# Decode attention on one core: value matmuls with the probabilities as stationary operand, and the maximum of a head taken ahead of the exponentials

## The chip, the cores and the metric

The kernel runs on one core of a Trainium2 chip. The metric is the device time of one execution in microseconds (us). The time of a kernel is the median of several runs; profiles come from one execution of their own. Engines are named as in the profile: PE (TensorE; PEld is its weight load), DVE (VectorE), ACT (ScalarE), POOL (GpSimd) and SP (SyncE, which here issues transfers). SBUF is the working memory, PSUM the memory that matmuls write.

## The reference, cut to what matters

A batch of 8 single tokens attends to a window of 2048 cached positions, with 32 query heads that share 8 K and V heads, and a small gated block scales the result:

```python
xn = _layernorm(x)                                   # x: 8 x 1 x 512
q = (xn @ wq).reshape(8, 1, 32, 128)
k = repeat(k_cache[:, :, -2048:, :], 4)              # cache: 8 x 8 x 8192 x 128, bf16
v = repeat(v_cache[:, :, -2048:, :], 4)
p = softmax(einsum("bhqd,bhkd->bhqk", q, k) * 128 ** -0.5)
s = einsum("bhqk,bhkd->bhqd", p, v).reshape(8, 1, 4096) @ wo
h = sigmoid(xn @ w_gate) * (xn @ w_up)               # 512 to 1792
return x + s * silu(h @ w_down)
```

All inputs are bf16. The windows of K and V are 67.1 MB of the 81.0 MB that are read, each element once.

## The kernel before, in words

**Tiles and transfers.** The K and the V window of one batch are each two tiles of four heads (2.1 MB a tile): 128 partitions hold 4 heads times 32 stretches of positions, and a partition holds 64 consecutive positions of 128 numbers. There are five K buffers and four V buffers. All loads go through SP's queue in one fixed order (`want_rows`, `want_cache`, lines 134 to 148): the block's weights and wq first, then K and V tiles in turn with V three tiles behind K, and wo in four pieces at the end, in K buffers. `pump` issues the head of that list as soon as its pool has room; a head without room holds up all that follow. `free` is called where the last instruction that reads a tile is emitted: for K after the last transpose of the tile, for V after the last value matmul on it.

**A batch** is handled in 16 steps of the loop at line 535; a unit `u` is two steps, four units make one K tile. In each step PE transposes eight 128x128 blocks of K (`k_transposes`, L343) and DVE copies them from PSUM (L348). `scores` (L362) multiplies them by the queries, in four column groups of the array, one for each K head: a query operand of 32 columns per head, 512 positions per matmul. A row of the score tile (128 x 512) is thus one head and one of four parts of its positions (index `j`), so a head is spread over four rows.

**Softmax before.** `row_max` (L376, L378) takes the maximum of each row, and ACT forms the exponentials of each row against this own maximum (L385), with the row's sum. `p_transposes` (L399, L404) turns the probabilities so that positions lie on the partitions. The four rows of a head have different maxima: `stat_rows`, `stat_weights`, `stat_sums` and `stat_factors` bring maxima and sums onto one partition, compute a factor for each row (L409 to L455), and `spread_factors` (L465, L473) copies the factors to all partitions by an fp32 matmul.

**Values before.** `values` (L485) handles one unit: 16 matmuls, each with a 128x128 block of V as the stationary operand and 16 columns of probabilities as the moving one, summed in PSUM. Each row has a result of its own; `normalise` (L499 to L516) multiplies by the factors, adds the four rows of a head and spreads the result, and `turn` (L526, L533) brings it into the layout of the output projection `fin` (L577). That projection runs once, after all batches: 128 matmuls in four column groups, then two DVE operations (L589, L591) and the store.

**Order of the work.** It is written out by hand (`manual_schedule`): the dictionary `tasks` says which functions are emitted in which step, after that step's K transposes, and each engine runs its instructions in that order. While batch b is loaded and scored, the row maxima of batch b-1 stand at step 2, its probabilities are turned at steps 8 and 9, its first V tile is used at steps 12 to 15, and the second V tile of batch b-2 at steps 5 to 8. So the first V tile of a batch comes free at step 15 of the next batch and the second at step 8 of the one after. After the last batch the loop makes one more round without K.

Of the kernel before, what the change touches and what calls it, by code (L numbers as in the profile page):

```python
# [10 lines left out]
def kernel(  # L11
# [13 lines left out]
    nc = tc.nc  # L25
# [90 lines left out]
    def free(tag):  # L116
        room[tag] += 1
        pump()
# [36 lines left out]
    make_identity(nc, ident[:])  # L155
    ident_f = consts.tile([P, P], f32, name="ident_f")
    make_identity(nc, ident_f[:])
    ones_row = consts.tile([1, P], f32, name="ones_row")
    nc.gpsimd.memset(ones_row[:], 1.0)

    perm = consts.tile([P, P], bf16, name="perm")
    nc.vector.tensor_copy(
# [157 lines left out]
            ),  # L320
        )


    free("k")
    free("k")

    oT_ps = ps_o.tile([P, 2, P], f32, name="oT_ps")

    kT = {}
    s_ps = {}  # L330
    pT = {}
    st = {}
    row = {}
    fac = {}

    def k_transposes(b, u, h):
        i, j = u // NJ, u % NJ
# [32 lines left out]
            )  # L370

    def row_max(b):
        st[b] = small.tile([P, 2], f32, name="st")
        nc.vector.reduce_max(out=st[b][:, 0:1], in_=s_ps[b][:], axis=AX.X)  # L376
        nb = small.tile([P, 1], f32, name="nb")
        nc.vector.tensor_scalar(  # L378
            out=nb[:], in0=st[b][:, 0:1], scalar1=-scale, scalar2=None, op0=ALU.mult
        )  # L380

        s = s_ps.pop(b)
        for l in range(G):
            rows = slice(NR * l, NR * (l + 1))
            nc.scalar.activation(  # L385
                out=p_buf[b % 2][rows, :, l, :],
                in_=s[rows, :].rearrange("k (c p) -> k p c", p=PG),
                func=AF.Exp,
                bias=nb[rows, :],
                scale=scale,  # L390
                accum_out=st[b][rows, 1:2],
            )

    def p_transposes(b, h):
        if h == 0:
            pT[b] = ppool.tile([P, CU, P], bf16, name="pT_sb")
        pT_ps = ps_t.tile([P, CH, P], bf16, name="pT_ps", tag="t")
        for c in range(CH):
            nc.tensor.transpose(  # L399
                out=pT_ps[:, c, :],  # L400
                in_=p_buf[b % 2][:, :, :, h * CH + c].rearrange("k p l -> k (p l)"),
                identity=ident[:],
            )
        nc.vector.tensor_copy(out=pT[b][:, h * CH : (h + 1) * CH, :], in_=pT_ps[:])  # L404

    def stat_rows(b):
        r = ps_m.tile([1, 2, P], f32, name="r_ps", tag="m")
        for k in range(2):
            nc.tensor.transpose(  # L409
                out=r[:, k, :], in_=st[b][:, k : k + 1], identity=ident_f[:]  # L410
            )
        row[b] = r
        del st[b]

    NH = NQ * rep

    def stat_weights(b):
        r = row[b]
        top = small.tile([1, G, NH], f32, name="top")
        nc.vector.reduce_max(  # L420
            out=top[:],
            in_=r[:, 0, :].rearrange("o (l j h) -> o l h j", l=G, j=NJ),
            axis=AX.X,
        )
        d = small.tile([1, G, NJ, NH], f32, name="d")
        nc.vector.tensor_tensor(  # L426
            out=d[:],
            in0=r[:, 0, :].rearrange("o (l j h) -> o l j h", l=G, j=NJ),
            in1=top[:].unsqueeze(2).to_broadcast([1, G, NJ, NH]),
            op=ALU.subtract,  # L430
        )
        w = small.tile([1, G, NJ, NH], f32, name="w")
        nc.scalar.activation(out=w[:], in_=d[:], func=AF.Exp, scale=scale)  # L433
        row[b] = (r, w)

    def stat_sums(b):
        r, w = row[b]
        wd = small.tile([1, G, NJ, NH], f32, name="wd")
        nc.vector.tensor_tensor(
            out=wd[:],  # L440
            in0=w[:],
            in1=r[:, 1, :].rearrange("o (l j h) -> o l j h", l=G, j=NJ),
            op=ALU.mult,
        )
        den = small.tile([1, G, NH], f32, name="den")
        nc.vector.reduce_sum(
            out=den[:], in_=wd[:].rearrange("o l j h -> o l h j"), axis=AX.X
        )
        row[b] = (w, den)

    def stat_factors(b):
        w, den = row[b]
        nc.vector.reciprocal(out=den[:], in_=den[:])
        f = small.tile([1, G, NJ, NH], f32, name="f")
        nc.vector.tensor_tensor(  # L455
            out=f[:],
            in0=w[:],
            in1=den[:].unsqueeze(2).to_broadcast([1, G, NJ, NH]),
            op=ALU.mult,
        )  # L460
        row[b] = f

    def spread_factors(b):
        f_ps = ps_m.tile([P, P], f32, name="f_ps", tag="m")
        nc.tensor.matmul(  # L465
            f_ps[:],
            lhsT=ones_row[:],
            rhs=row.pop(b)[:].rearrange("o l j h -> o (l j h)"),
            start=True,
            stop=True,  # L470
        )
        fac[b] = small.tile([P, P], f32, name="fac")
        nc.scalar.copy(out=fac[b][:], in_=f_ps[:])  # L473

    def values(b, u):
        i, j = u // NJ, u % NJ
        v_sb = v_tiles[(b, i)]

        def cols(ap):
            return ap.rearrange("p (l j i r) -> p l j i r", l=G, j=NJ, i=NQ)[  # L480
                :, :, j, i, :
            ]

        for c in range(CU):
            nc.tensor.matmul(  # L485
                cols(oT_ps[:, b % 2, :]),
                lhsT=v_sb[:, j * CU + c, :],
                rhs=cols(pT[b][:, c, :]),
                start=(c == 0),
                stop=(c == CU - 1),  # L490
            )
        if j == NJ - 1:
            del v_tiles[(b, i)]
            free("v")

    def normalise(b):
        del pT[b]
        t = small.tile([P, G, NJ, NQ, rep], f32, name="on")
        nc.vector.tensor_tensor(  # L499
            out=t[:].rearrange("p l j i r -> p (l j i r)"),  # L500
            in0=oT_ps[:, b % 2, :],
            in1=fac.pop(b)[:],
            op=ALU.mult,
        )
        oT = small.tile([P, Hq], bf16, name="oT")
        with nc.allow_low_precision(reason="operand of the next matmul"):
            for i in range(NQ):
                nc.vector.reduce_sum(  # L508
                    out=oT[:, i * G * rep : (i + 1) * G * rep].rearrange(
                        "p (l r) -> p l r", l=G  # L510
                    ),
                    in_=t[:, :, :, i, :].rearrange("p l j r -> p l r j"),
                    axis=AX.X,
                )
        oB = small.tile([P, Hq, NDQ], bf16, name="oB")
        nc.vector.tensor_tensor(  # L516
            out=oB[:],
            in0=oT[:].unsqueeze(2).to_broadcast([P, Hq, NDQ]),
            in1=band[:].unsqueeze(1).to_broadcast([P, Hq, NDQ]),
            op=ALU.mult,  # L520
        )
        row[b] = oB

    def turn(b):
        oP_ps = ps_m.tile([P, RT], f32, name="oP_ps", tag="m")
        nc.tensor.matmul(  # L526
            oP_ps[:],
            lhsT=row.pop(b)[:].rearrange("p h q -> p (h q)"),
            rhs=pick[:],
            start=True,  # L530
            stop=True,
        )
        nc.scalar.copy(out=oP_sb[:, :, b], in_=oP_ps[:])  # L533

    for b in range(B + 1):
        now = b if b < B else None
        pb = b - 1 if b >= 1 else None
        pp = b - 2 if b >= 2 else None
        tasks = {s: [] for s in range(2 * NU + 1)}
        if now is not None:  # L540
            for u in range(NU - 1):
                tasks[2 * u + 3].append(lambda u=u: scores(now, u))
        if pb is not None:
            tasks[1].append(lambda: scores(pb, NU - 1))
            tasks[2].append(lambda: row_max(pb))
            tasks[8].append(lambda: p_transposes(pb, 0))
            tasks[9].append(lambda: p_transposes(pb, 1))
            tasks[8].append(lambda: stat_rows(pb))
            tasks[9].append(lambda: stat_weights(pb))
            tasks[11].append(lambda: stat_sums(pb))  # L550
            tasks[12].append(lambda: stat_factors(pb))
            if b < B:
                tasks[15].append(lambda: spread_factors(pb))
            for u in range(NJ):
                tasks[12 + u].append(lambda u=u: values(pb, u))
        if pp is not None:
            for u in range(NJ, NU):
                tasks[5 + u - NJ].append(lambda u=u: values(pp, u))
            tasks[9].append(lambda: normalise(pp))
            tasks[13].append(lambda: turn(pp))  # L560
        for s in range(2 * NU + 1):
            if now is not None and s < 2 * NU:
                k_transposes(now, s // 2, s % 2)
            for f in tasks[s]:
                f()
    spread_factors(B - 1)
    for u in range(NJ, NU):
        values(B - 1, u)
    normalise(B - 1)
    turn(B - 1)  # L570

# [55 lines left out]
```

## Time and profile before

| what | value |
|---|---|
| median of 3 runs | 203.11 us (202.01 to 203.39) |
| the profiled execution | 202.38 us, span 200.2 us, mean granted clock 0.88 |
| PE, PEld | 155.0 us (77%), 124.0 us (62%) |
| DVE, ACT | 129.6 us (65%), 38.2 us (19%) |
| K transposes L343 / their copies L348 | 76.9 / 83.4 us |
| value matmuls L485, weight loads | 34.8 us x1024, 31.5 us |
| scores L362 | 26.2 us x256 |
| transfers | 81.41 MB, mean 407 GB/s |

The span is the profiled part of an execution; the execution's own time is 2.2 us longer. In the rows of slices each digit is the busy share of one fortieth of the span, in tenths; PEclk is the clock that PE was granted, in tenths of full speed. In the chain, a line has the start, the length and what ran, and the chain is followed back from the last instruction. The mean time of one matmul in a group is its time from start to end, while matmuls overlap: what a matmul adds in a stream is read from the chain or from the length of a group divided by its number.

### The profile page before, as it was taken

The page shows a single profiled execution, that of the slowest core. Times are in us where ns is not written, and L with a number is a line of the kernel's source. Part 1 is how long each engine was busy: PE and PEld are TensorE (multiplying, and loading weights), DVE is VectorE, ACT ScalarE, POOL GpSimd, SP SyncE. Part 2 cuts the span into 40 slices and gives each one's busy share as a digit, 9 for nine tenths or more (in the row PEclk, how much of TensorE's full clock was granted, in tenths as well). Part 3 has the DMA queues.
Part 4 walks back from the last instruction along what each step waited for, and adds up shares of the span by engine and source line. Part 5 has one row for each costly group of instructions (what it writes and reads, how often), then busy time and mean ns, then how long its engine had stood idle before and what let it go on. Part 6 is the DMA issues. An engine that isn't in the chain of part 4 may idle for free.

```text
span 200.2 us, 6209 instructions
## 1 busy us (share of the span) xinstructions
PE 155.0 (77%) x2838; PEld 124.0 (62%) x2838; DVE 129.6 (65%) x272; ACT 38.2 (19%) x97; POOL 1.3 (1%) x9
## 2 busy tenths in 40 slices
PE   0397057999699989878987998889688978885763
PEld 0144057676577877667766876767477767765662
DVE  4824005899698798838873887697549873961621
ACT  5040000004402401601060106010501060023100
POOL 2000000000000000000000000000000000000000
PEclk9999555899999999979997899999969996995558
DMA  6999999999999999999999999999999999999940
GB/s 211 438 424 438 432 425 425 439 429 424 425 429 435 422 429 425 429 435 425 432 422 429 439 422 425 425 432 429 429 425 425 432 435 422 425 425 425 419 195 7
DMA packets 6009, 81.41 MB, mean 407 GB/s; under 512 B 728, under 2 KB 736, under 8 KB 864
## 3 DMA queue, kind: packets, MB, share of 16 engines
q1 hardware_dynamic: 5936, 81.01, 95.3%
q8 instruction: 22, 0.36, 0.7%
q14 instruction: 3, 0.02, 0.0%
q10 hardware_dynamic: 48, 0.01, 0.0%
HBM read 81.01 MB, written 0.01 MB: 405 GB/s over the span
## 4 chain that ended last, share of the span: by engine, by line
DMA 70%; PE 18%; DVE 6%; ACT 2%; SPq 2%; issue 1%; ACTq 0%; DVEq 0%
DMA k_sb<-in_A_k_cache_dram 70%; PE kT_ps L343 8%; PE oT_ps L485 3%; PE pT_ps L399 2%; PE s_ps L362 2%; DVE kT_sb L348 2%; PE fin_ps L577 2%; ACT p_buf L385 2%; SPq L99 1%; DVE pT_sb L404 1%; DVE st L376 1%; PE r_ps L409 1%; PE f_ps L465 1%; DVE oT L508 0%; DVE on L499 0%
## 5 line engine op out<-in xcount | busy, mean ns | idle before, releaser
L348 DVE COPY kT_sb<-kT_ps 128x1024 bf16<-128x1024 bf16 x128 | 83.4, 683 | 27.3 <-PE kT_ps L343 26.8
L343 PE MATMUL kT_ps<-perm,k_sb 128*128 128x128 bf16 x1024 | 76.9, 227 | 9.9 <-DMA k_sb<-in_A_k_cache_dram 9.9
L343 PEld LDWEIGHTS <-k_sb 128*128 128x128 bf16 x1024 | 62.4, 102 | 17.6 <-DMA k_sb<-in_A_k_cache_dram 10.5
L485 PEld LDWEIGHTS <-v_sb 128*128 128x128 bf16 x1024 | 31.5, 98 | 9.1 <-issue 6.2
L485 PE MATMUL oT_ps<-pT_sb,v_sb 128*128 128x16 bf16 x1024 | 34.8, 171 | 2.5 <-DVE on L499 1.5
L362 PE MATMUL s_ps<-kT_sb,qm_sb 128*32 128x512 bf16 x256 | 26.2, 399 | 7.0 <-DVE kT_sb L348 6.2
L385 ACT ACTIVATE p_buf<-s_ps,nb 32x512 bf16<-32x512 f32 x32 | 21.7, 679 | 24.0 <-DVE nb L378 23.7
L404 DVE COPY pT_sb<-pT_ps 128x1024 bf16<-128x1024 bf16 x16 | 11.0, 689 | 10.6 <-PE pT_ps L399 10.6
L399 PE MATMUL pT_ps<-ident,p_buf 128*128 128x128 bf16 x128 | 13.4, 262 | 4.6 <-ACT p_buf L385 4.6
L362 PEld LDWEIGHTS <-qm_sb 128*32 128x32 bf16 x256 | 8.3, 93 | 13.5 <-issue 6.4
L399 PEld LDWEIGHTS <-p_buf 128*128 128x128 bf16 x128 | 11.0, 156 | 6.8 <-ACT p_buf L385 4.8
L433 ACT ACTIVATE w<-d 1x128 f32<-1x128 f32 x8 | 2.5, 309 | 50.2 <-DVE d L426 50.2
L308 PE MATMUL qT_ps<-xnT_sb,wq_sb 128*128 128x8 bf16 x128 | 3.7, 168 | 7.0 <-DMA wq_sb<-in_A_wq_dram 7.0
L308 PEld LDWEIGHTS <-wq_sb 128*128 128x128 bf16 x128 | 3.6, 104 | 7.3 <-DMA wq_sb<-in_A_wq_dram 7.3
L233 PE MATMUL g_ps<-wg_sb,xnT_sb 128*8 128x448 bf16 x16 | 5.3, 509 | 3.2 <-DMA wg_sb<-in_B_w_gate_dram 3.2
L316 DVE CAST qm_sb<-qT_ps 128x32 bf16<-128x32 f32 x8 | 0.9, 182 | 10.2 <-PE qT_ps L308 10.2
L385 ACT ACT_TABLE_LOAD x1 | 1.3, 1283 | 27.7 <-DVE nb L378 27.7
L533 ACT CAST oP_sb<-oP_ps 128x32 bf16<-128x32 f32 x8 | 2.4, 300 | 21.0 <-PE oP_ps L526 21.0
L385 ACT ACTIVATION_READ_ACCUMULATOR p_buf<-s_ps,nb 32x1 f32 x32 | 5.9, 184 | 0.0
L376 DVE TENSOR_REDUCE st<-s_ps 128x1 f32<-128x512 f32 x8 | 5.5, 682 | 0.5 <-PE s_ps L362 0.5
L233 PEld LDWEIGHTS <-xnT_sb 128*8 128x8 bf16 x16 | 1.8, 115 | 6.3 <-issue 5.6
L473 ACT COPY fac<-f_ps 128x128 f32<-128x128 f32 x8 | 2.1, 266 | 17.2 <-PE f_ps L465 17.2
(62 smaller groups left out, 71.9 us busy)
## 6 DMA issues: line engine op xcount, KB each, us to landing
k_sb<-in_A_k_cache_dram SPq DMA_DIRECT2D x16, 2048.0 KB, 36.5
v_sb<-in_A_v_cache_dram SPq DMA_DIRECT2D x16, 2048.0 KB, 33.2
wq_sb<-in_A_wq_dram SPq DMA_DIRECT2D x2, 2048.0 KB
wo_sb<-in_A_wo_dram SPq DMA_DIRECT2D x2, 1024.0 KB, 21.4
wg_sb<-in_B_w_gate_dram SPq DMA_DIRECT2D x1, 1792.0 KB, 7.4
wu_sb<-in_B_w_up_dram SPq DMA_DIRECT2D x1, 1792.0 KB
wd_sb<-in_B_w_down_dram SPq DMA_DIRECT2D x1, 1792.0 KB
wo_sb<-in_A_wo_dram SPq DMA_DIRECT2D x1, 1536.0 KB, 19.7
```

The costliest lines, as they stand in the source:

```text
L233: nc.tensor.matmul(g_ps[:], lhsT=xnT_sb[:, kt, :], rhs=weights[("wg_sb", kt)][:, k * FC : (k + 1) * FC], start=(kt == 0), stop=(kt == KT - 1),
L308: nc.tensor.matmul(qT_ps[:, h * B : (h + 1) * B], lhsT=weights[("wq_sb", kt)][:, h * Dh : (h + 1) * Dh], rhs=xnT_sb[:, kt, :], start=(kt = ...
L343: nc.tensor.transpose(out=kT_ps[:, c, :], in_=k_sb[:, j * CU + h * CH + c, :], identity=perm[:],)
L348: nc.vector.tensor_copy(out=kT[(b, u)][:, h * CH : (h + 1) * CH, :], in_=kT_ps[:])
L362: nc.tensor.matmul(s_ps[b][NR * l : NR * (l + 1), :], lhsT=qm_sb[:, b, i * G + l, o : o + Z], rhs=t[:, :, PG * l : PG * (l + 1)], start=(u ...
L376: nc.vector.reduce_max(out=st[b][:, 0:1], in_=s_ps[b][:], axis=AX.X)
L385: nc.scalar.activation(out=p_buf[b % 2][rows, :, l, :], in_=s[rows, :].rearrange("k (c p) -> k p c", p=PG), func=AF.Exp, bias=nb[rows, :], ...
L399: nc.tensor.transpose(out=pT_ps[:, c, :], in_=p_buf[b % 2][:, :, :, h * CH + c].rearrange("k p l -> k (p l)"), identity=ident[:],)
L404: nc.vector.tensor_copy(out=pT[b][:, h * CH : (h + 1) * CH, :], in_=pT_ps[:])
L433: nc.scalar.activation(out=w[:], in_=d[:], func=AF.Exp, scale=scale)
L485: nc.tensor.matmul(cols(oT_ps[:, b % 2, :]), lhsT=v_sb[:, j * CU + c, :], rhs=cols(pT[b][:, c, :]), start=(c == 0), stop=(c == CU - 1),)
L577: nc.tensor.matmul(fin_ps[Z * j : Z * (j + 1), :], lhsT=oP_sb[:, t, :], rhs=weights[("wo_sb", t)][:, j * P : (j + 1) * P], start=(t == 0), ...
```

## The change

It changes the softmax's statistics, the value matmuls and the order of both.

- The maximum of a head, over its four rows, is formed ahead of the exponentials: DVE takes the row maxima, PE turns them onto one partition (`stat_rows`), DVE takes the maximum of four and scales it, an fp32 matmul with one column brings it back to the rows (`spread_max`), and ACT copies it and then forms the exponentials. All rows of a head now share one scale, and the factors per row are gone.
- The sums of the rows are added and spread by an fp32 matmul against ones (`sums`), in one layout with the result.
- A value matmul has the probabilities as the stationary operand (32 columns: the rows of one tile and two of the four parts) and 256 columns of V as the moving one: two position blocks side by side, of which the rows of the fitting part are used. Four such matmuls, one in each column group of the array, cover both V tiles of a batch at one `c`; 16 values of `c` make a batch. The transposes of the probabilities take a permuted identity (`turn_rows`), which sorts the rows into those groups.
- The result lies with rows on partitions. `combine` copies it from PSUM on ACT, and `normalise` adds the four rows of a head and turns the result by two fp32 matmuls with a selection matrix (`sel_out`). Both matrices and `turn_rows` are made once, on DVE.
- In the order of the work, the statistics of batch b-1 stand at steps 2, 4 and 6 (before: 8 to 15), its turned probabilities at 11 and 12, and all values of batch b-2 at steps 6 to 13, after which both of its V tiles come free. The round after the last batch is written out; there the values of the last batch are formed one tile after the other.

```diff
+    Hh = G * rep
+    turn_rows = consts.tile([P, P], bf16, name="turn_rows")
+    sel_den = consts.tile([P, Hq], f32, name="sel_den")
+    sel_out = consts.tile([P, 2, Hq], f32, name="sel_out")
...
-    oT_ps = ps_o.tile([P, 2, P], f32, name="oT_ps")
+    o_ps = ps_o.tile([P, 2, 2 * Dh], f32, name="o_ps")
+    m_ps = ps_m.tile([P, 2, 256], f32, name="m_ps", tag="m")
...
     def row_max(b):
-        st[b] = small.tile([P, 2], f32, name="st")
-        nc.vector.reduce_max(out=st[b][:, 0:1], in_=s_ps[b][:], axis=AX.X)
+        st[b] = small.tile([P, 1], f32, name="st")
+        nc.vector.reduce_max(out=st[b][:], in_=s_ps[b][:], axis=AX.X)
+
+    def stat_rows(b):
+        nc.tensor.transpose(out=r_ps[b % 2], in_=st.pop(b)[:], identity=ident_f[:])
+        top = small.tile([1, G, NH], f32, name="top")
+        nc.vector.reduce_max(
+            out=top[:],
+            in_=r_ps[b % 2].rearrange("o (l j h) -> o l h j", l=G, j=NJ),
+            axis=AX.X,
+        )
+        row[b] = small.tile([1, G, NJ, NH], f32, name="neg")
+        nc.vector.tensor_scalar(
...
+        )
+
+    def spread_max(b):
+        nc.tensor.matmul(
+            nb_ps[b % 2],
+            lhsT=row.pop(b)[:].rearrange("o l j h -> o (l j h)"),
+            rhs=ones_sq[0:1, 0:1],
+            start=True,
+            stop=True,
+        )
         nb = small.tile([P, 1], f32, name="nb")
-        nc.vector.tensor_scalar(
-            out=nb[:], in0=st[b][:, 0:1], scalar1=-scale, scalar2=None, op0=ALU.mult
-        )
+        nc.scalar.copy(out=nb[:], in_=nb_ps[b % 2])
...
-                identity=ident[:],
+                identity=turn_rows[:],
...
-    def stat_weights(b):
...
-    def stat_sums(b):
...
-    def stat_factors(b):
...
-    def spread_factors(b):
...
-    def values(b, u):
...
+    def sums(b):
+        own = small.tile([P, Hq], f32, name="own")
+        nc.vector.tensor_scalar(
+            out=own[:],
+            in0=sel_den[:],
+            scalar1=st.pop(b)[:],
+            scalar2=None,
+            op0=ALU.mult,
+        )
+        nc.tensor.matmul(
+            den_ps[b % 2], lhsT=ones_sq[:], rhs=own[:], start=True, stop=True
+        )
+        den = small.tile([P, Hq], f32, name="den")
+        nc.vector.reciprocal(out=den[:], in_=den_ps[b % 2])
+        inv[b] = small.tile([P, Hq, NDQ], f32, name="inv")
...
+    def values(b, c, tiles=range(NQ)):
+        for i in tiles:
+            v = v_tiles[(b, i)][:].rearrange("p (m e c) d -> p m c e d", e=2, c=CU)
+            for m in range(NJ // 2):
+                k = i * (NJ // 2) + m
+                rows = slice(32 * k, 32 * (k + 1))
+                nc.tensor.matmul(
+                    o_ps[rows, b % 2, :].rearrange("k (e d) -> k e d", e=2),
+                    lhsT=pT[b][:, c, rows],
+                    rhs=v[:, m, c],
+                    start=(c == 0),
+                    stop=(c == CU - 1),
+                    tile_position=(0, 32 * k),
+                    skip_group_check=True,
+                )
+            if c == CU - 1:
+                del v_tiles[(b, i)]
+                free("v")
+
+    def combine(b):
...
+        nc.scalar.copy(
+            out=o[:], in_=o_ps[:, b % 2, :].rearrange("k (e d) -> k e d", e=2)
+        )
...
     def normalise(b):
...
+        for e in range(2):
             nc.tensor.matmul(
...
+                oT_ps[b % 2],
+                lhsT=o[:, e, :],
+                rhs=sel_out[:, e, :],
+                start=(e == 0),
+                stop=(e == 1),
+            )
...
+            tasks[2].append(lambda: row_max(pb))
+            tasks[4].append(lambda: stat_rows(pb))
+            tasks[6].append(lambda: spread_max(pb))
+            tasks[11].append(lambda: p_transposes(pb, 0))
+            tasks[12].append(lambda: p_transposes(pb, 1))
+            tasks[13].append(lambda: sums(pb))
         if pp is not None:
+            for c in range(CU):
+                tasks[6 + c // 2].append(lambda c=c: values(pp, c))
+            tasks[14].append(lambda: combine(pp))
+            tasks[15].append(lambda: normalise(pp))
+        if b >= 3:
+            tasks[1].append(lambda: turn(b - 3))
...
+    scores(B - 1, NU - 1)
+    turn(B - 3)
+    row_max(B - 1)
+    for c in range(CU):
+        if c == CU // 4:
+            stat_rows(B - 1)
+        if c == CU // 2:
+            spread_max(B - 1)
+        values(B - 2, c)
+    combine(B - 2)
+    p_transposes(B - 1, 0)
+    p_transposes(B - 1, 1)
+    normalise(B - 2)
+    sums(B - 1)
+    turn(B - 2)
+    for i in range(NQ):
+        for c in range(CU):
+            values(B - 1, c, (i,))
+    combine(B - 1)
     normalise(B - 1)
     turn(B - 1)
```

More of the change, by code (lines that the diff above doesn't have):

```diff
@@ L157 @@
     make_identity(nc, ident_f[:])
-    ones_row = consts.tile([1, P], f32, name="ones_row")
-    nc.gpsimd.memset(ones_row[:], 1.0)
+    ones_sq = consts.tile([P, P], f32, name="ones_sq")
+    nc.gpsimd.memset(ones_sq[:], 1.0)
     perm = consts.tile([P, P], bf16, name="perm")
@@ L325 @@
     free("k")
-    oT_ps = ps_o.tile([P, 2, P], f32, name="oT_ps")
+    Hh = G * rep
[3 more added lines that the diff above has]
+    for i in range(NQ):
+        nc.vector.tensor_copy(
+            out=turn_rows[:].rearrange("k (i j l r) -> k i j l r", i=NQ, j=NJ, l=G)[
+                :, i
+            ],
+            in_=ident[:].rearrange("k (l j i r) -> k i j l r", i=NQ, j=NJ, l=G)[:, i],
+        )
+        nc.vector.reduce_sum(
+            out=sel_den[:, i * Hh : (i + 1) * Hh].rearrange("k (l r) -> k l r", l=G),
+            in_=ident_f[:].rearrange("k (l j i r) -> k i l r j", l=G, j=NJ, i=NQ)[:, i],
+            axis=AX.X,
+        )
+    for e in range(2):
+        nc.vector.reduce_sum(
+            out=sel_out[:, e, :].rearrange("k (i h) -> k i h", i=NQ),
+            in_=ident_f[:].rearrange(
+                "k (i m e h) -> k e i h m", i=NQ, m=NJ // 2, e=2
+            )[:, e],
+            axis=AX.X,
+        )
+    o_ps = ps_o.tile([P, 2, 2 * Dh], f32, name="o_ps")
+    m_ps = ps_m.tile([P, 2, 256], f32, name="m_ps", tag="m")
+    r_ps = [m_ps[0:1, x, 0:P] for x in range(2)]
+    nb_ps = [m_ps[:, x, 128:129] for x in range(2)]
+    den_ps = [m_ps[:, x, 136 : 136 + Hq] for x in range(2)]
+    oT_ps = [m_ps[:, x, 168 : 168 + Hq] for x in range(2)]
+    oP_ps = [m_ps[:, x, 200 : 200 + RT] for x in range(2)]
     kT = {}
@@ L333 @@
     row = {}
-    fac = {}
+    inv = {}
     def k_transposes(b, u, h):
@@ L370, in scores @@
             )
+    NH = NQ * rep
     def row_max(b):
-        st[b] = small.tile([P, 2], f32, name="st")
-        nc.vector.reduce_max(out=st[b][:, 0:1], in_=s_ps[b][:], axis=AX.X)
+        st[b] = small.tile([P, 1], f32, name="st")
[6 more added lines that the diff above has]
+            in_=r_ps[b % 2].rearrange("o (l j h) -> o l h j", l=G, j=NJ),
+            axis=AX.X,
+        )
+        row[b] = small.tile([1, G, NJ, NH], f32, name="neg")
+        nc.vector.tensor_scalar(
+            out=row[b][:],
+            in0=top[:].unsqueeze(2).to_broadcast([1, G, NJ, NH]),
+            scalar1=-scale,
+            scalar2=None,
[9 more added lines that the diff above has]
+        )
         nb = small.tile([P, 1], f32, name="nb")
-        nc.vector.tensor_scalar(
-            out=nb[:], in0=st[b][:, 0:1], scalar1=-scale, scalar2=None, op0=ALU.mult
-        )
+        nc.scalar.copy(out=nb[:], in_=nb_ps[b % 2])
         s = s_ps.pop(b)
+        st[b] = small.tile([P, 1], f32, name="sums")
         for l in range(G):
@@ L390, in row_max @@
                 scale=scale,
-                accum_out=st[b][rows, 1:2],
+                accum_out=st[b][rows, :],
             )
@@ L401, in p_transposes @@
                 in_=p_buf[b % 2][:, :, :, h * CH + c].rearrange("k p l -> k (p l)"),
-                identity=ident[:],
+                identity=turn_rows[:],
             )
         nc.vector.tensor_copy(out=pT[b][:, h * CH : (h + 1) * CH, :], in_=pT_ps[:])
[L406 to L413, printed above, removed]
@@ L415 @@
-    NH = NQ * rep
-    def stat_weights(b):
[L418 to L423, printed above, removed]
-        )
-        d = small.tile([1, G, NJ, NH], f32, name="d")
-        nc.vector.tensor_tensor(
[L427 to L434, printed above, removed]
@@ L436, in stat_sums @@
-    def stat_sums(b):
[L437 to L442, printed above, removed]
+    def sums(b):
[4 more added lines that the diff above has]
+            scalar1=st.pop(b)[:],
+            scalar2=None,
+            op0=ALU.mult,
+        )
+        nc.tensor.matmul(
[4 more added lines that the diff above has]
+        inv[b] = small.tile([P, Hq, NDQ], f32, name="inv")
+        nc.vector.tensor_tensor(
+            out=inv[b][:],
+            in0=den[:].unsqueeze(2).to_broadcast([P, Hq, NDQ]),
+            in1=band[:].unsqueeze(1).to_broadcast([P, Hq, NDQ]),
@@ L443, in stat_sums @@
             op=ALU.mult,
         )
-        den = small.tile([1, G, NH], f32, name="den")
-        nc.vector.reduce_sum(
-            out=den[:], in_=wd[:].rearrange("o l j h -> o l h j"), axis=AX.X
-        )
-        row[b] = (w, den)
-    def stat_factors(b):
[L452 to L461, printed above, removed]
@@ L463, in spread_factors @@
-    def spread_factors(b):
[L464 to L473, printed above, removed]
-    def values(b, u):
[L476 to L490, printed above, removed]
-            )
-        if j == NJ - 1:
-            del v_tiles[(b, i)]
-            free("v")
@@ L496, in normalise @@
[L496 to L514, printed above, removed]
+    def values(b, c, tiles=range(NQ)):
[16 more added lines that the diff above has]
+                free("v")
@@ new lines, in combine, with normalise @@
+    def combine(b):
+        del pT[b]
+        o = small.tile([P, 2, Dh], f32, name="o_sb")
+        nc.scalar.copy(
+            out=o[:], in_=o_ps[:, b % 2, :].rearrange("k (e d) -> k e d", e=2)
+        )
+        row[b] = o
+    def normalise(b):
+        o = row.pop(b)
+        for e in range(2):
+            nc.tensor.matmul(
+                oT_ps[b % 2],
[3 more added lines that the diff above has]
+                stop=(e == 1),
+            )
@@ L517, in normalise @@
             out=oB[:],
-            in0=oT[:].unsqueeze(2).to_broadcast([P, Hq, NDQ]),
-            in1=band[:].unsqueeze(1).to_broadcast([P, Hq, NDQ]),
+            in0=oT_ps[b % 2].unsqueeze(2).to_broadcast([P, Hq, NDQ]),
+            in1=inv.pop(b)[:],
             op=ALU.mult,
@@ L524, in turn @@
     def turn(b):
-        oP_ps = ps_m.tile([P, RT], f32, name="oP_ps", tag="m")
         nc.tensor.matmul(
-            oP_ps[:],
+            oP_ps[b % 2],
             lhsT=row.pop(b)[:].rearrange("p h q -> p (h q)"),
@@ L532, in turn @@
         )
-        nc.scalar.copy(out=oP_sb[:, :, b], in_=oP_ps[:])
-    for b in range(B + 1):
-        now = b if b < B else None
+        nc.scalar.copy(out=oP_sb[:, :, b], in_=oP_ps[b % 2])
+    for b in range(B):
         pb = b - 1 if b >= 1 else None
         pp = b - 2 if b >= 2 else None
[L539 to L542, printed above, removed]
+        tasks = {s: [] for s in range(2 * NU)}
+        for u in range(NU - 1):
+            tasks[2 * u + 3].append(lambda u=u: scores(b, u))
         if pb is not None:
@@ L545 @@
             tasks[2].append(lambda: row_max(pb))
[L546 to L555, printed above, removed]
-        if pp is not None:
[L557 to L563, printed above, removed]
+            tasks[4].append(lambda: stat_rows(pb))
[3 more added lines that the diff above has]
+            tasks[13].append(lambda: sums(pb))
+        if pp is not None:
+            for c in range(CU):
[4 more added lines that the diff above has]
+            tasks[1].append(lambda: turn(b - 3))
+        for s in range(2 * NU):
+            k_transposes(b, s // 2, s % 2)
             for f in tasks[s]:
                 f()
-    spread_factors(B - 1)
-    for u in range(NJ, NU):
-        values(B - 1, u)
+    scores(B - 1, NU - 1)
[13 more added lines that the diff above has]
+    turn(B - 2)
+    for i in range(NQ):
+        for c in range(CU):
+            values(B - 1, c, (i,))
+    combine(B - 1)
     normalise(B - 1)
```

## The prediction, made before the changed kernel ran

> **What bounds the kernel now.** I read the slices of the page first, then the chain that ended last, then the last microseconds by window.
>
> ```profile
> PEclk9999555899999999979997899999969996995558
> DMA  6999999999999999999999999999999999999940
> ...
> HBM read 81.01 MB, written 0.01 MB: 405 GB/s over the span
> ```
>
> The DMA row stands at 9 from the second slice to the 38th: the 16 engines are full from about 5 to 190 us, and PE, at 77%, waits for them. Where it waits is in the chain:
>
> ```profile
> 128.06 37.99 DMA k_sb<-in_A_k_cache_dram
> ...
> 166.10 1.03 PE kT_ps L343 x8
> ...
> 179.12 0.77 ACT p_buf L385 x2
> ...
> 189.53 1.82 PE oT_ps L485 x64
> ...
> 193.19 3.63 PE fin_ps L577 x96
> ```
>
> The last K tile lands at 166.05. From there the chain is compute: transposes and scores, the last exponentials (179.12 to 182.25), value matmuls (to 191.35), the output projection (193.19 to 196.82); another 3.4 us end the span. But the transfers end at almost the same time:
>
> ```profile
> wo_sb<-in_A_wo_dram SPq DMA_DIRECT2D x1, 512.0 KB, 25.0
> ```
>
> This last piece of wo is issued at 171.0, so it lands at 196.0. The windows agree:
>
> ```profile
> 195.00:196.00 1.00, 1.00 (x48) 1.00 (x44) 0.00 (x0) 0.00 (x0) 0.00 (x0) 0.50 0.13 33
> 196.00:197.00 1.00, 0.79 (x32) 0.52 (x20) 0.16 (x1) 0.00 (x0) 0.00 (x0) 0.63 0.00 0
> ```
>
> Columns here are PE, PEld, DVE, ACT, POOL, clock, DMA share, GB/s. The projection takes 3.63/128 = 28.4 ns a matmul; its last 16, on that piece, take 0.45 us, so no order of the compute could end before 196.45. That is 0.37 us ahead of what was measured: **two ends of nearly equal length**. A change in compute can gain a few tenths and lose without limit.
>
> **The change, part by part.** First the stream of transfers. Four V buffers hold two batches. Before, they come free at step 15 of the next batch and step 8 of the one after; now both at step 13 of the one after, and SP is one queue in fixed order, so K tiles wait behind them. From K tile to K tile is 9.9 us (the K waits of the chain end at 86.2, 125.7 and 166.05, two batches or 39.7 us apart). At the step 8 whose K tile has just landed, four tiles (V, K, V, K; 19.8 us) are still issued. Before, steps 8 to 13 took 166.1 to 174.8, cold start included; so new issues come 8.8 us later, with 11 us queued. **Cost in the middle: nothing.** If a batch took over 19.8 us of compute this cover would shrink, but PE now rests 1.5 to 2 us a batch.
>
> At the end of the list only V of batch 6 follows the last K. 12.58 MB in 166.05 to 196.0 is 420 GB/s, so those two tiles land at 176.0. V of batch 7 and wo, issued from 168.86 on before, now wait for step 13 of batch 7: I get 175.0, plus 0.54 (an issue on SP), plus about 1 us to the first data (estimate: first issue at 0.74, windows near full rate from 3 us on, so 0.5 to 2). Bubble 0.5 us, bounds 0 and 2. New floor: 196.45 + 0.5 = 196.95.
>
> In the loop, PE loses 128 value matmuls a batch (28 to 31 ns each by the chain, 3.8 us) and gets 64 of 256 columns, in fours. The nearest row is L362, four 512-column matmuls in four column groups: 0.33 us by the chain. Half of that bounds a four of 256 columns at 0.17 us, the projection's rate (4 x 28.4 ns for 128 columns at clock 0.50) gives 0.11 at full clock: 16 fours are 1.8 to 2.7 us. Four fp32 matmuls and one transpose (nearest row f_ps, 0.41 us a pair of passes) replace one and two; DVE drops seven operations of 0.26 to 0.37 (d, wd, den's sum, f, on, two oT) and gets own and inv at about 0.28. So a batch gains about 1 us, and nothing comes of it: the next K tile is not there earlier. The exponentials start at step 6 instead of 2, 3.1 us, done ahead of the transposes now at 11. The first exponentials now wait for DVE, PE, DVE, PE, ACT; behind spread_max on PE stand step 7's transposes, with K's wait as cover. Behind the wait of the sums matmul for own (DVE, after a 0.68 us copy) stand the last values of step 13, hence V's release: 0.7 us, in my 175.0. Six small DVE operations at the start (about 1.4 us) fit between 31.57, the end of the casts, and the first copy at 33.05. Nothing.
>
> Whether switching between tiled and untiled matmuls costs anything: 0.33 us for a four against 4 x 28.4 x 4 / 2 = 0.23 leaves at most 0.10 us a visit; eight visits a batch are 0.8 us, inside the cover, and the tail has three more, 0.3 us, of which I take none. The Trainium skill, TensorEngine Tiling (Array Packing), Key Properties, says that changing the tiling mode drains TensorE; by that rule the sum would be up to 0.3 us higher, and the 0.10 us neither shows nor excludes it.
>
> **The end of the compute**, from 166.1. Steps 8 to 13 to 174.9: six groups of K transposes (two cold at 1.0, four at 0.5), three scores (0.33, cold 0.45), six value groups (0.23, cold 0.45), two pT groups (0.51), the 0.7 wait and the sums' 0.3, with 0.5 in waits for DVE. Steps 14 and 15, scores and normalise to 177.4: 0.7 earlier than the 178.1 before. Row maximum 0.7 (178.15). Then new: transpose and its latency 0.35, top 0.27, neg 0.28, matmul 0.3, copy 0.25: exponentials start at 179.6 and end at 182.75, **0.5 later** than before. pT 2.0 (1.07 + 0.92 by the chain, cold), normalise 0.9, oB and own 0.5, sums 0.4, turn 0.2: value matmuls of batch 7 start at 186.75. There the new form is dear: a tile at a time, so only two of four column groups work. 32 pairs of 256 columns by the projection's rate are 32 x 0.227 = 7.3 us at clock 0.50 and 3.6 at full, against 128 x 28 ns = 3.6 before, whose time did not hang on the clock. The clock rows decide:
>
> ```profile
> 32.00:33.00 1.00, 1.00 (x10) 1.00 (x11) 0.00 (x0) 0.00 (x0) 0.00 (x0) 0.50 1.07 459
> ...
> 36.00:37.00 1.00, 1.00 (x19) 0.95 (x16) 0.48 (x2) 0.00 (x0) 0.00 (x0) 0.84 0.96 410
> ...
> 190.00:191.00 1.00, 1.00 (x44) 1.00 (x41) 0.00 (x0) 0.00 (x0) 0.00 (x0) 0.50 0.81 336
> ```
>
> After a rest the clock came back 4.2 us into dense work (31.98 to 36.2) and 3.5 into the projection; the 16-column matmuls up to 191.35 did not bring it back. PE rests from 180.2 to 182.75 for the exponentials, so I start values cold, full after 4.2 us: 4.2 + (1 - 4.2/7.3) x 3.6 = 5.7 us, to 192.5. (The Trainium skill, TensorE: Matmul & The Clock Gate, Part 1, has one free-running window of about 3.4 us; by that the wait lies between 3.4 and 6.8 us and values take 5.4 to 7.1; the trace's 3.5 and 4.2 fit.) Then copy 0.45, normalise 0.8, oB 0.3, turn 0.2, cast 0.3, gaps 0.3: projection from 194.85. At 3.63 us cold or 1.8 at full clock; after 2.4 us of near rest I take 3.2. End 198.05 against 196.82: **+1.2 us**, above the floor. Span 201.4; with the 2.2 us outside the span (202.38 - 200.2) the profiled execution becomes 203.6. The median of the runs shown stands 0.7 above it, so **204.3 us**. About 1% (2 us) is what a measurement of this kernel can tell from no change.
>
> **Rivals.**
> - The tail hides. Clock back at once and kept: values 3.9, projection 1.8, end 194.7, then the last wo piece decides at 196.95: 203.1 to 203.4. For it: pT and normalise ahead of the values are nearly dense. Against: the same stretch ran at 0.50 before. 0.22.
> - Slower. The clock stays at half through values and projection: values to 194.1, projection from 196.5 to 200.1: +3.3, 206.4. It decides once PE's rest between 180 and 183 takes the clock and the work up to 190.2 is too thin to return it: slices 37 to 39 of the page are 5 5 5. 0.22.
> - Slower too: transfers starve. V released late in every batch costs the stream what is beyond the 11 us; 1 us in each of five batches is 208. Against: PE's rests. 0.07.
> - The stream itself gets quicker, or the projection ends at the floor on a stream without bubble (202.7). A time under 201.1 needs an end at 194.8, before the last weights have landed at 420 GB/s. 0.04.
> - My forecast, 203.4 to 205.5: 0.45.
>
> That the change does not do what it says I hold small: the maximum is shared ahead of the exponentials and row factors go, in any case.
>
> **Numbers.** Range 202.6 to 207.0: from the stream's floor with the spread of the runs, up past the cold rival with fp32 matmuls at the cold 0.76 of f_ps. Faster by over 1% 0.04; within, 0.58 (the hidden tail and most of the forecast); slower 0.38 (the two slow rivals, and the upper end of the forecast).
>
> **What would show it.** DMA at 9 through slice 37, and the waits for K about 39.7 us apart: the middle is free. SP issuing V of batch 7 at about 175, not 169; last exponentials ending near 182.8; the last value stage 5 to 7 us long with the clock at 0.50 in its first part; projection ending near 198. Wrong if PE waits for V inside a batch, if fp32 matmuls on the tail take over 0.8 us each, or if the last K tile lands later than 167.

## The result, and the profile after

The changed kernel takes 203.66 us (median of 16 runs, 203.37 to 206.28) against 202.71 for the kernel before (16 runs, 202.01 to 203.82): a ratio of **1.0063**, 95% interval 1.0033 to 1.0092. That is slower, and within the 1% that the prediction took as no change. The profiled execution took 203.39 us with a span of 201.2, 1.0 us more than before on both counts.

The slices of the changed kernel, in the order of the page:

```profile
PEclk9999555899999999969997999999958999996678
DMA  6999999999999999999999999999999999499980
GB/s 215 430 425 436 433 420 436 430 427 422 430 440 423 427 427 436 423 427 436 423 427 427 443 420 433 433 414 433 427 436 420 433 436 410 186 414 410 426 370 5
```

In the DMA row the 35th slice, 171 to 176 us, is a 4 (186 GB/s) where there was a 9. The 39th is an 8 where there was a 4, since the transfers end later. Up to the 34th slice the stream is as full as before, and PE waited for K about as long as before. The first line is the kernel before, the second the changed one (time in all, times, longest):

```profile
PE kT_ps L343 <- DMA k_sb<-in_A_k_cache_dram: 9.9, 7, 2.2
```

```profile
PE kT_ps L376 <- DMA k_sb<-in_A_k_cache_dram: 10.4, 6, 2.5
```

The chain that ended last, in order of time, shows what that hole does (start, length, what ran):

```profile
146.12 0.05 issue
146.16 1.03 PE kT_ps L376 x8
...
173.70 0.33 PE o_ps L495 x8
174.03 1.01 PE kT_ps L376 x16
175.05 0.20 SPq L89
...
176.99 20.30 DMA wo_sb<-in_A_wo_dram
197.29 0.04 issue
197.33 0.43 PE fin_ps L598 x16
```

Before, the chain ran through the last exponentials, the value matmuls and the projection. Now it leaves PE at 175: the last value matmuls of step 13 (L495, 173.70 to 174.03) release the V tiles, SP issues the last V tiles and wo, and the chain ends with the landing of wo at 197.29, 1.3 us later than the 196.0 of before. In both kernels 16 matmuls need that last piece. From 146.16 to 175 the chain is compute without a wait for K, so the pace of the compute from the middle of batch 6 on sets the time of the release. In the timeline of the same stretch, PE stands waiting in the middle of the projection (the bracket is idle time, and what ended it):

```profile
185.76 5.20 PE L495 MATMUL o_ps<-v_sb,pT_sb 128*32 128x256 bf16 x64
193.07 2.21 PE L598 MATMUL fin_ps<-wo_sb,oP_sb 128*32 128x128 bf16 x80 [0.39 <-ACT oP_sb L543]
196.11 0.87 PE L598 MATMUL fin_ps<-wo_sb,oP_sb 128*32 128x128 bf16 x32 [0.82 <-DMA wo_sb<-in_A_wo_dram]
197.33 0.41 PE L598 MATMUL fin_ps<-wo_sb,oP_sb 128*32 128x128 bf16 x16 [0.35 <-DMA wo_sb<-in_A_wo_dram]
```

The projection starts at 193.07, 0.12 us earlier than before (193.19). Without the two waits, the 3.63 us that the projection took before would have ended at 196.7, where the kernel before ended (196.82). The compute is not longer; the transfers end later.

The windows around the hole (the last three columns are clock, DMA share, GB/s):

```profile
171.00:172.00 1.00, 1.00 (x21) 0.72 (x20) 0.99 (x2) 0.00 (x0) 0.00 (x0) 1.00 0.65 279
172.00:173.00 1.00, 0.69 (x11) 0.29 (x8) 0.90 (x2) 0.00 (x0) 0.00 (x0) 1.00 0.55 229
173.00:174.00 1.00, 0.71 (x11) 0.46 (x12) 0.50 (x3) 0.00 (x0) 0.00 (x0) 1.00 0.31 131
174.00:175.00 1.00, 1.00 (x24) 0.90 (x20) 0.76 (x3) 0.37 (x1) 0.00 (x0) 1.00 0.08 33
175.00:176.00 1.00, 0.96 (x13) 0.71 (x12) 0.95 (x3) 0.00 (x0) 0.00 (x0) 1.00 0.88 262
```

From 171 on the DMA share falls from window to window, as it would if one DMA engine after another ran out of work; at 174 to 175 it is that of little more than one of 16. SP's first issue is at 174.06, and in windows of 0.2 us nothing moves from 174.4 to 175.4; then the stream starts again.

So there are two readings. **Theory A**: the late release of V in the last batch decides, and nothing else in the change costs time. **Theory B**, the forecast's own: the new form of the value matmuls and what follows it lengthen the compute at the end, and the landing of wo comes second. In this one profile A's end is 1.1 us later than B's (197.76 against 196.7), about as much as the whole change in time, so it needs a test.

### The profile page after: what moved, and what is told of

It reads as the page before. It is cut to its first block, busy times and chain, and to the rows that moved or that the text cites. A ratio compares the mean times of both kernels' runs of the same rounds, so it can differ in the third digit from the quotient of the medians.

```text
span 201.2 us, 5246 instructions
## 1 busy us (share of the span) xinstructions
PE 157.6 (78%) x2366; PEld 110.4 (55%) x2366; DVE 122.9 (61%) x238; ACT 37.9 (19%) x97; POOL 1.3 (1%) x9
## 4 chain that ended last, share of the span: by engine, by line
DMA 67%; PE 25%; SPq 3%; DVE 3%; issue 1%
DMA k_sb<-in_A_k_cache_dram 57%; PE kT_ps L376 14%; DMA wo_sb<-in_A_wo_dram 10%; PE o_ps L495 5%; PE s_ps L395 3%; PE pT_ps L458 2%; SPq L99 2%; DVE kT_sb L381 2%; SPq L89 1%; PE m_ps L475 1%; DVE st L410 0%; DVE own L468 0%; PE m_ps L519 0%; PE fin_ps L598 0%; PE m_ps L430 0%
## 5 line engine op out<-in xcount | busy, mean ns | idle before, releaser
L376 PE MATMUL kT_ps<-perm,k_sb 128*128 128x128 bf16 x1024 | 78.5, 228 | 10.4 <-DMA k_sb<-in_A_k_cache_dram 10.4
L495 PE MATMUL o_ps<-v_sb,pT_sb 128*32 128x256 bf16 x512 | 28.3, 304 | 0.0
L495 PEld LDWEIGHTS <-pT_sb 128*32 128x32 bf16 x512 | 12.3, 102 | 6.6 <-issue 2.3
L511 ACT COPY o_sb<-o_ps 128x256 f32<-128x256 f32 x8 | 3.0, 372 | 58.8 <-PE o_ps L495 58.8
L458 PE MATMUL pT_ps<-turn_rows,p_buf 128*128 128x128 bf16 x128 | 11.0, 230 | 3.6 <-ACT p_buf L444 3.6
L458 PEld LDWEIGHTS <-p_buf 128*128 128x128 bf16 x128 | 9.3, 150 | 5.6 <-ACT p_buf L444 4.1
L395 PEld LDWEIGHTS <-qm_sb 128*32 128x32 bf16 x256 | 6.7, 93 | 7.0 <-issue 0.8
L475 PE MATMUL m_ps<-own,ones_sq 128*128 128x32 f32 x16 | 3.5, 302 | 5.2 <-DVE own L468 5.2
L475 PEld LDWEIGHTS m_ps<-own,ones_sq 128*128 128x128 f32 x16 | 2.6, 203 | 7.4 <-DVE own L468 7.4
L527 DVE TENSOR_TENSOR oB<-m_ps,inv 128x128 bf16<-128x128 f32 x8 | 2.3, 292 | 6.6 <-PE m_ps L519 6.2
L543 ACT CAST oP_sb<-m_ps 128x32 bf16<-128x32 f32 x8 | 2.4, 301 | 21.1 <-PE m_ps L536 21.1
```

The costliest lines, as they stand in the source:

```text
L376: nc.tensor.transpose(out=kT_ps[:, c, :], in_=k_sb[:, j * CU + h * CH + c, :], identity=perm[:],)
L395: nc.tensor.matmul(s_ps[b][NR * l : NR * (l + 1), :], lhsT=qm_sb[:, b, i * G + l, o : o + Z], rhs=t[:, :, PG * l : PG * (l + 1)], start=(u ...
L458: nc.tensor.transpose(out=pT_ps[:, c, :], in_=p_buf[b % 2][:, :, :, h * CH + c].rearrange("k p l -> k (p l)"), identity=turn_rows[:],)
L475: nc.tensor.matmul(den_ps[b % 2], lhsT=ones_sq[:], rhs=own[:], start=True, stop=True)
L495: nc.tensor.matmul(o_ps[rows, b % 2, :].rearrange("k (e d) -> k e d", e=2), lhsT=pT[b][:, c, rows], rhs=v[:, m, c], start=(c == 0), stop=( ...
L511: nc.scalar.copy(out=o[:], in_=o_ps[:, b % 2, :].rearrange("k (e d) -> k e d", e=2))
```

## The experiments

The ratios are to the kernel before, with 95% intervals, and the runs of the kernel before were shared within the first four experiments and within the last three.

### The release alone, two steps earlier

```diff
-                tasks[6 + c // 2].append(lambda c=c: values(pp, c))
+                tasks[(4 if b == B - 1 else 6) + c // 2].append(lambda c=c: values(pp, c))
```

> The changed kernel with one edit: in the last round of the loop the values of batch 5 stand at steps 4 to 11 instead of 6 to 13, so that the last two V tiles and wo are issued about two steps (2.2 to 2.5 us) earlier. Theory A (late release: in the profile of the changed kernel the stream of transfers fell to 33 GB/s at 174 to 175 and the last piece of wo landed at 197.3 instead of 196.0): V of batch 7 is issued near 171.7, the dip shrinks to nothing, wo lands near 196.0, and the time is 0.7 to 1.3 us below the changed kernel's 203.66, 0.998 to 1.002 of before. Theory B (my forecast: the value matmuls of the last batch and what follows them set the end): the tail of the compute is not touched, the time stays at 1.006 of before.

Measured: **0.9973** (0.9956 to 0.9989), 202.08 us. SP issued the last V tiles from 170.14 on instead of 174.06, which is 3.9 us earlier and not the 2.2 to 2.5 expected, and wo from 171.37 on instead of 175.29; the last piece of wo landed at 196.0 (issued at 173.5, 22.5 us to landing). The projection of this kernel no longer waits for it:

```profile
185.73 5.71 PE o_ps L495 x59
...
193.54 3.15 PE fin_ps L598 x128
```

The gain on the changed kernel is 0.9%, a little more than A expected (0.998 of before at best), and A holds. The edit also lets the last row maximum start earlier (175.62 instead of 176.41), but the projection starts no earlier for it (193.54 instead of 193.07), so the gain does not come from the compute. The rest of the change is then even slightly faster than the kernel before.

### The late release alone, in the kernel before

```diff
+    def release(b):
+        hold = ps_m.tile([P, RT], f32, name="hold", tag="m")
+        for i in range(NQ):
+            nc.tensor.matmul(
+                hold[:],
+                lhsT=v_tiles.pop((b, i))[:, 0, :],
+                rhs=pick[:],
...
+            free("v")
...
             tasks[9].append(lambda: normalise(pp))
+            tasks[13].append(lambda: release(pp))
             tasks[13].append(lambda: turn(pp))
```

The lines that freed V in `values` are gone.

> The kernel before with the late release alone: both V tiles of a batch are held by one further small matmul each at step 13 of the batch two later; values, softmax and order stay as they were. Theory A: V of batch 7 is issued near 175, the stream dips, the last piece of wo lands 0.8 to 1.5 us later than 196.0, and the time is 1.003 to 1.007 of before. Theory B: the compute of before is not longer by more than 0.1 us, the time is 1.000 of before (0.998 to 1.002).

Measured: **1.0076** (1.0051 to 1.0102), 204.09 us: a little more than the changed kernel lost. The chain of its profile is the changed kernel's, with the small matmul in the place of the values:

```profile
174.61 0.08 PE hold L495 x2
...
177.60 20.53 DMA wo_sb<-in_A_wo_dram
198.13 0.04 issue
198.17 0.64 PE fin_ps L586 x16
```

The last piece of wo lands 2.1 us later than in the kernel before, more than the 1.5 expected at most, and the time is a little above the 1.007 expected at most. SP's first issue is 0.6 us later here than in the changed kernel (174.67 against 174.06), and from 175 to 176 nothing moves (DMA share 0.00). The late release stands in every batch of this kernel, and DMA is at nine through slice 34 all the same. The two parts multiply to 0.9973 x 1.0076 = 1.0049, near the 1.0063 of the whole.

### A part of wo ahead of the last V tiles

```diff
+        if n == len(order) + 1:
+            want_rows("wo_sb", A_wo, "k", RT, 0, 8)
...
-    for t0, t1 in ((0, 12), (12, 20), (20, 28), (28, 32)):
+    for t0, t1 in ((8, 16), (16, 24), (24, 32)):
```

> The changed kernel with the list of loads changed: the first eight of the 32 rows of wo (1.05 MB, 2.5 us at 420 GB/s) stand ahead of the last two V tiles and so are issued with V of batch 6; the release stays at step 13. Theory A: these 2.5 us fill the dip of 1.3 us, the stream ends near 196.0 and the time falls by 0.6 to 1.2 us against the changed kernel, to 0.999 to 1.003 of before; V of batch 7 lands up to 1.2 us later, which the values of the last batch may feel on their second tile. Theory B: nothing is gained, 1.006, or 1.010 where the later V holds up the values.

Measured: **1.0014** (0.9984 to 1.0044), 202.66 us. The release still came at step 13, with SP's issue at 173.8, but the DMA row now has an 8 where there was a 4. The last piece landed at 195.3 (176.2 plus 19.1), and the projection, from 193.06 on, ran without a wait. This speaks for the stream running dry, and not the release itself, as what costs time. As a gain in time it is likely rather than clear: four of the twelve runs took 203.4 to 204.2, as long as the changed kernel's, and the interval overlaps a little with that of the whole change.

### The values of the last batch in four column groups

```diff
-    for i in range(NQ):
-        for c in range(CU):
-            values(B - 1, c, (i,))
+    for c in range(CU):
+        values(B - 1, c)
```

> The changed kernel with the values of the last batch formed over both V tiles at once, in four column groups as in the loop, instead of one tile after the other in two: 64 matmuls in 16 fours, 3.6 us at half clock and 1.8 at full against the 5.2 measured. Theory B (that stage sets the end): 1.5 us less than the changed kernel, 0.999 of before. Theory A: the start now waits for the second V tile (issued at 174.65, landing near 187.5 against a start at 185.8), the stage ends no earlier than 190.7 and wo still lands near 197.3: no gain, 1.005 to 1.008 of before.

Measured: **1.0063** (1.0040 to 1.0086), 203.72 us: no gain, as A said. The stage waits for the second V tile and then for wo:

```profile
188.00 3.37 PE L495 MATMUL o_ps<-v_sb,pT_sb 128*32 128x256 bf16 x62 [2.00 <-DMA v_sb<-in_A_v_cache_dram]
...
197.73 0.62 PE L597 MATMUL fin_ps<-wo_sb,oP_sb 128*32 128x128 bf16 x16 [0.19 <-DMA wo_sb<-in_A_wo_dram]
```

This also shows what the order "one tile after the other" in the change is good for: with a late second tile it lets PE start 2 us sooner.

### Both: earlier release and four column groups

> Both edits at once: in the last round the values of batch 5 stand two steps earlier (as in the first experiment, 0.9973 of before, whose compute ended at 196.69 while wo landed near 196.0), and the values of the last batch are formed in 16 fours. Theory A, both ends count: the compute now ends earlier (last V tile landing near 184.5, fours 3.4 to 3.6 us at half clock, projection from 191.5), so the last piece of wo decides at 196.0 plus 0.45: 0.2 to 0.3 us less than the first experiment, 0.994 to 0.998 of before. If the tail of the compute alone set the end, 2 us less: 0.988.

Measured: **0.9945** (0.9921 to 0.9970), 201.39 us, the fastest of all. The compute is now done first, and wo decides again:

```profile
194.02 1.04 PE L597 MATMUL fin_ps<-wo_sb,oP_sb 128*32 128x128 bf16 x32 [1.10 <-DMA wo_sb<-in_A_wo_dram]
195.26 0.62 PE L597 MATMUL fin_ps<-wo_sb,oP_sb 128*32 128x128 bf16 x16 [0.20 <-DMA wo_sb<-in_A_wo_dram]
```

The last piece lands at 195.2 (173.8 plus 21.4). The stage that B held for dear, 5.71 us in the first experiment, takes 3.09 here, yet the gain over that experiment is about 0.3%, with intervals that overlap: two ends of nearly equal length, as the prediction read them, with the compute a little behind in the one and the stream in the other. Part of that gain is the stream's: wo landed at 196.0 there and at 195.2 here, though V was issued at nearly the same time (170.14 and 170.39).

### More work for PE in the middle

In the first experiment's kernel, eight transposes of K are done twice in two steps of each of batches 1 to 6.

```diff
+        again = CH if 1 <= b <= 6 and (2 * u + h) in (2, 10) else 0
-        for c in range(CH):
+        for c in list(range(again)) + list(range(CH)):
             nc.tensor.transpose(
```

> The first experiment's kernel with more work for PE in the middle: in batches 1 to 6, at steps 2 and 10, the eight transposes of K are done twice (1.0 us a batch at full clock, 6 us in all; the output is the same). Theory A with the cover of the prediction (PE rests 1.5 to 2 us a batch in front of the next K tile): no change, 0.996 to 1.000 of before. If PE's time in the loop counts, up to 6 us: 1.02 or more; if only the last batches count, through a later release of V, 1.000 to 1.004.

Measured: **0.9962** (0.9944 to 0.9980), 201.71 us: no slower than the 0.9973 without the extra 6 us. From the waits of the first experiment and of this one (time in all, times, longest):

```profile
PE kT_ps L376 <- DMA k_sb<-in_A_k_cache_dram: 10.8, 6, 4.1
```

```profile
PE kT_ps L377 <- DMA k_sb<-in_A_k_cache_dram: 8.9, 6, 2.4
```

The extra work shortened PE's rests in front of the next K tile, and the mean granted clock rose from 0.892 to 0.923. In batches 1 to 6, and with the early release, 6 us more of PE's time cost nothing. For the changed kernel's own last batches this is not shown: there the chain runs through the compute from 146 on.

### The release one step later

```diff
-                tasks[6 + c // 2].append(lambda c=c: values(pp, c))
+                tasks[(7 if b == B - 1 else 6) + c // 2].append(lambda c=c: values(pp, c))
```

> The changed kernel with its values of batch 5 one step later in the last round (steps 7 to 14), so that the last V tiles and wo are issued about 1.1 us later, near 175.2. Theory A: every us of lateness past the point at which the stream runs dry is a us at the end: wo lands near 198.3 and the time is 0.7 to 1.2 us over the changed kernel's, 1.009 to 1.013 of before. Theory B: the same time as the changed kernel, 1.006, since the compute tail has the same length.

Measured: **1.0142** (1.0099 to 1.0184), 205.55 us. The stream stands still for two windows:

```profile
175.00:176.00 1.00, 1.00 (x24) 0.57 (x16) 0.77 (x3) 0.00 (x0) 0.00 (x0) 1.00 0.00 0
176.00:177.00 1.00, 1.00 (x17) 0.65 (x13) 0.81 (x2) 0.37 (x1) 0.00 (x0) 1.00 0.00 0
```

The last V tile was issued at 176.76 instead of 174.65, 2.1 us later rather than the 1.1 expected, and wo landed at 199.79 instead of 197.29, 2.5 later. Its projection starts at 195.11; without the waits it would have ended by 198.8 instead of 200.47. Lateness at this point is paid in full, and the time lies a little above the 1.013 that A expected at most.

Only 0.9 of the 2.1 us are the later step. The other 1.2 are there by step 13, whose value matmuls start at 174.88 instead of 173.70: in this profile PE rested 2.77 us in front of the last K tile and began step 8, at 165.49, at half clock, while in the changed kernel's it came to that step without a wait and at full clock.

```profile
165.00:166.00 1.00, 0.51 (x5) 0.51 (x6) 0.00 (x0) 0.00 (x0) 0.00 (x0) 0.57 1.07 459
166.00:167.00 1.00, 1.00 (x13) 0.40 (x11) 0.43 (x1) 0.00 (x0) 0.00 (x0) 0.50 0.84 360
```

```profile
166.00:167.00 1.00, 1.00 (x21) 0.63 (x18) 0.69 (x1) 0.97 (x4) 0.00 (x0) 1.00 0.95 393
```

The first two lines are this run's, the third is the changed kernel's.

## Why the prediction was right, and where it was not

The time was right: 204.3 against 203.11 is a ratio of 1.0058, measured 1.0063, and the profiled execution was forecast at 203.6 and took 203.39. The sum behind it was not: of its two ends, it held the wrong one for the later. That the total fits is luck. The end of the compute was forecast 1.3 us too late (198.05 against 196.7 without the waits), the end by the stream 0.8 too early (196.95 against 197.76), and the later of the two forecasts lies 0.3 us from the later of the two ends. Its own signs could not tell the two apart: the projection did end near 198, and the value stage did take 5 to 7 us.

- **The middle costs nothing: right.** DMA at nine through slice 34; PE's waits for K were 9.9 us before and 10.4 after, no wait for V is left, and 6 us of added work in the first experiment's kernel changed nothing. A batch gained what was reckoned: eight value matmuls take 0.22 to 0.33 us in the chain, 1.8 to 2.6 us a batch at full clock against 3.8 before, which lies in the forecast 1.8 to 2.7.
- **The late release: mechanism right, size wrong.** The step that failed is "Bubble 0.5 us": the landing of wo moved by 1.3, which lies inside the stated bounds of 0 and 2 but puts the stream's end behind the compute's. The issue was forecast well, even too late (175.0 and 0.54; measured 174.06 for the first V tile and 174.65 for the second). But only the slowest engine was counted, with one figure for its end (176.0). The stream does not run dry all at once: from 170 to 178 the DMA shares lack 2.8 us of full stream (the sum of what each window lacks of 1, with 1.30 in one window counted against it). The taper at the end, 3.3 us of missing share from 190 to 196 before, is 1.7 after (194 to 197.3). 2.8 + 1.7 - 3.3 = 1.2, about the 1.3 measured. Why the taper is shorter is not shown: the two kernels of the fifth and sixth experiments, which have no hole, end with 2.2 to 2.3 and land at 195.2.
- **The compute at the end: +1.2 forecast, about -0.1 measured** (196.7 without the waits against 196.82). Two terms were too large. Steps 8 to 13 were taken from 166.1 with a cold start, as before (their terms add up to 9.2 us, so to 175.3 and not the 174.9 written); PE went through step 8 at 165.62 at full clock, so that the last row maximum began at 176.41 instead of 177.45. And the value stage took 5.2, not 5.7. The start of the exponentials was late against the row maximum by even more than reckoned (1.65 us from its end, not 1.45). The transposes of the probabilities were taken at the cold rate, 2.0 us, and took 1.06, since the clock fell only at 183; that saved little, for from their start to the value matmuls it was 3.84 us against a forecast of 4.0, with DVE's copies and small operations in between.
- **The value stage's dependence on the clock: right, and of no effect.** It ran at half clock until about 189.8, 4.1 us after its start (4.2 forecast). It could not decide, because the stream ended later anyway. That the two figures agree is partly luck: in the profiles with the same stage the clock came back after 3.9 us (sixth experiment), 4.7 (third), 5.2 (first) and 5.4 (seventh), and the stage took 5.10, 5.65, 5.76 and 5.92 us. From these five, the stage would take about 3.1 us at full and 6.3 at half clock (an estimate), less than the forecast's 3.6 and 7.3. The Trainium skill, TensorE: Matmul & The Clock Gate, Part 1, has a free-running window of about 3.4 us; an estimate from it puts the return of the clock 3.4 to 6.8 us after a start, and these five traces agree, while in the fourth experiment it came back 3.0 us after PE went on at 188.0 from a rest of 2.0.
- **The rival "the tail hides"** comes nearest to what happened: the compute was done in time and the last piece of wo decided. Its 203.1 to 203.4 was too low by the rest of the bubble. The rival of starving transfers came true in the last batch alone, and the forecast had that part in its own floor.

What stays open: three of the 16 runs of the changed kernel took 205.2 to 206.3 us, and the others 203.4 to 203.8. The late release could give such a spread, since PE's pace in the last batches then counts in full, and the seventh experiment's profile, itself one of the longer of its runs (206.12 of 203.99 to 206.50), shows a way: a rest and a cold start at the last K tile, worth 1.2 us. The spreads alone do not show it. Kernels with the late release stay within 1.4 us too (second and fourth experiment), and the kernel before, without it, spreads over 2.4. No profile of such a run of the changed kernel was taken.

## What to carry to other kernels

Where a stream of transfers is the bound, look first at what a change does to the time at which buffers come free, at the end of the list of loads above all: in the middle other tiles were in flight and gave 11 us of cover by the prediction's reckoning, at the end only two were left, and a release 3.9 us earlier or 2.1 us later took 0.9% off the time or put 0.8% on it. Work out both ends, that of the transfers and that of the compute, and which one is later with its uncertainty: here they lay 1.1 us apart, and the total came out right with the wrong one ahead. An order written by hand can be mended for its last round alone: the two small edits of the fifth experiment make the changed kernel the slightly faster one (0.9945 of before).

## What the runs showed of the hardware

- A hole in the stream moves its end by less than the missing share, by the bookkeeping of these profiles: 2.8 us moved it by 1.3, since the taper at the end was shorter (1.7 instead of 3.3). How much of that the hole itself does is open, as kernels without a hole have tapers from 2.2 to 3.3.
- A visit to column-tiled matmuls has a price on both sides. In the chain of the changed kernel at full clock, eight value matmuls take 0.33 us right after transposes, and 0.22 right after scores, which are tiled as well. And the transposes behind a visit take longer: eight take 0.55 and sixteen 1.00, but 0.89 for sixteen after the untiled fp32 matmuls of `normalise`:

```profile
68.45 0.33 PE s_ps L395 x4
68.78 0.22 PE o_ps L495 x8
69.00 0.55 PE kT_ps L376 x8
69.55 0.33 PE o_ps L495 x8
...
157.17 1.00 PE kT_ps L376 x16
...
158.50 0.56 PE m_ps L519 x4
159.06 0.89 PE kT_ps L376 x16
```

That is 0.11 us going in, the 0.10 that the prediction could only bound, and about as much again coming out. The Trainium skill, TensorEngine Tiling (Array Packing), Key Properties, says that a change of tiling mode drains TensorE; the trace agrees that a change costs time, 0.11 us each way, but does not show what the time is spent on.
- More work for PE can pay for a part of itself: with twelve groups of transposes done twice the mean granted clock was 0.906 to 0.931 over twelve runs instead of 0.892 to 0.912 over twelve. In the two profiles PE's longest rest in front of a K tile was 2.4 us instead of 4.1, which is the likely reason.
